# First scores ahead of the keys' second part, whole gathered rows scaled, and one last scatter, in a fused attention and MoE kernel

## The chip, the cores and the metric

One of the eight cores of a Trainium2 chip runs the whole program. A core has five engines with an instruction queue each: TensorE (PE, matmul; its weight loads are listed as PEld), VectorE (DVE), ScalarE (ACT), GpSimd (POOL) and SyncE (SP, which here only issues transfers). The metric is the time of one execution in device microseconds (us). Lower is better.

## The reference

An attention with keys and values pooled over eight neighbours, and behind it a mixture of experts in which each token goes to one expert (cut):

```python
batch, n_heads, seq, head_dim = (8, 8, 576, 64)
k_p = k.reshape(B, H, Sp, pool, D).mean(axis=3)      # Sp = 72, pool = 8
v_p = v.reshape(B, H, Sp, pool, D).mean(axis=3)
scores = scale * np.matmul(q, k_p.transpose(0, 1, 3, 2))
attn = softmax(scores)
x = np.matmul(attn, v_p)                             # as [4608 tokens, 512]
...
logits = x @ w_gate + modality_bias[modality_id]     # 8 experts
e_idx = np.argmax(logits, axis=1)
gate_w = softmax(logits)[arange(N), e_idx]
for e in range(E):                                   # w1 512x1024, w2 1024x512
    h = np.maximum(x[mask] @ w1[e], 0.0)
    out[mask] = gate_w[mask, None] * (h @ w2[e])
```

## The kernel before, in words

**Attention.** The 8 batches of 576 queries are worked through in 20 steps; each takes the rows of 256 tokens or so, five steps for every two batches, and has two halves of four heads (`sc_0`, `sc_1`). A half's life: query rows are transposed on PE (`pq`, L508) and copied by ACT (`qt`); PE makes the scores (`sc`, L533; L527 where a step spans two batches); DVE takes the maximum (`mx`, L540) and subtracts it (`sb`, L543); ACT takes the exponential (`pe`, L555, L556); PE transposes it (`pp`, L562, and `sc` L574 for the last columns) and ACT copies it (`pt`, L567, L581); PE multiplies with the pooled values (`av`, L597, L601), where the gate's logits and the sum of the exponentials come along as extra columns; DVE and ACT divide and write the rows (`xb`, L603 to L642); SP stores them to DRAM (`xs`).

Keys and values arrive in chunks (`c`) of 128 pooled rows and a rest `k4`, `v4`. The sum over eight neighbours is taken either by DVE in one reduction (`reduce8`, L309) or by POOL in three folding additions (`fold`, L304 to L306). PE transposes the key sums (`pk`, L340, L343) in two parts; `kt` is the scores' operand. The values' sums become `vw`, an operand for `av`.

The order of all this is written by hand. A prologue issues the loads on SP's queue and does the first sums and transposes; then each step runs a fixed sequence on PE, with places (`hook_0` to `hook_3`, `hook_q`) at which the next batch's sums and operands are called. Every engine works its own queue in that order, so an instruction that waits holds all behind it. The program before makes the first scores behind both parts of the keys of batch 0, and all key sums of batch 1's first part plus the second part's stand together on DVE.

In the late groups (the route is computed in four groups of steps; two are early) half of each token row is copied raw by ACT and is divided only after gathering, by POOL, the other half by DVE at once. The divisors travel in the row as extra columns.

**Experts.** Tokens are sorted by expert into slots of 256 rows, 18 fixed and up to 27 if the data need it; slots from index 18 on are under conditions (`more`, L1267 to L1285). With these data 19 slots are used and the last has 109 rows, so that a shorter end (`end_half`) runs. A slot: POOL gathers the two tiles of 128 rows from DRAM (`xg`, L143, an indirect DMA), multiplies half of each row by its divisors (`scale_half`, L148 to L153), PE transposes the rows (`xt`, L155 to L164). Then eight blocks f = 0 to 7 of 128 hidden units: PE makes `hp` (L170), ACT and DVE the rectified `hh` and its remainder `hlo`, PE the output `op` (L1155); meanwhile ACT and DVE split the next weights into two parts (`hl`, L136, L139). The results are scaled by the gate's weight into `ob` (DVE, ACT; L1132 to L1143) and scattered by POOL to `out` (L1141), which is done in the next slot's f = 0. Gathers for the next slot are issued there too, slot 2's at f = 3 of slot 1, behind slot 0's scatters. Scale and transposes come at f = 3 and f = 5 (slot 1: 5 and 6).

**End.** Behind the conditions stand two scatters of the rows in `obl` (L1288 to L1291), the first of them zeros when the last slot is half full. Each waits for the other's landing. Then the program ends (L1317).

Of the kernel before, what the change touches and what calls it, by code (L numbers as in the profile page):

```python
# [22 lines left out]
P = 128  # L23
# [7 lines left out]
def kernel(  # L31
# [116 lines left out]
    def scale_half(s, xgs):  # L148
        for tt in range(2):
            x = xgs[(2 * s + tt) % len(xgs)]  # L150
            xv = x[:, 0:D // 2].rearrange("p (h d) -> p h d", h=H // 2)
            nc.gpsimd.tensor_tensor(xv, xv, x[:, RX:RX + H // 2].rearrange("p (h o) -> p h o", o=1).to_broadcast([P, H // 2, HD]),  # L152
                                    op=ALU.mult)  # L153
# [37 lines left out]
    with ExitStack() as actx:  # L191
# [64 lines left out]
        load_q(0, (1,))  # L256
        load_v(0)
        load_v4(0)
# [55 lines left out]
        def pool_k(b, parts=(0, 1)):  # L314
# [5 lines left out]
            for i in parts:  # L320
                cs = K_PART[i]
                if b == 0 or (b == 1 and i == 0):
# [4 lines left out]
                else:  # L327
                    for c in range(cs[0], cs[-1] + 1, 2):
                        m = min(c + 2, cs[-1] + 1)
                        fold(t[:, c:m], kp[:, c:m])  # L330
                    if i == 1:
                        fold(t4, kp4)

        def k_operand(b, i):
# [4 lines left out]
            for j, c in enumerate(cs):  # L339
                nc.tensor.transpose(pk[:, j * P:(j + 1) * P], kp[:, c, :], ident)  # L340
            n = len(cs) * P
# [7 lines left out]
        def pool_v(b):  # L349
            vp = ap.tile([P, NPAIR, HD], F32, tag="vp", bufs=2, name=f"vp_{b}")  # L350
            vp4 = ap.tile([P, HD], F32, tag="vp4", bufs=2, name=f"vp4_{b}")
            t, t4 = vraw[b], v4raw[b]
            fold(t[:, 0:2], vp[:, 0:2])
            if b:
                fold(t[:, 2:4], vp[:, 2:4])
            else:
                for j in range(2, NPAIR):
                    reduce8(t[:, j, :], vp[:, j, :])
            fold(t4, vp4)
            vps[b] = (vp, vp4)  # L360

# [241 lines left out]
        def x_dve(t):  # L603
# [5 lines left out]
            if gi == 0:  # L609
# [7 lines left out]
            late = g >= EARLY_GROUPS  # L617
# [8 lines left out]
            nc.vector.tensor_tensor(xo[:, D // 2:D].rearrange("p (h d) -> p h d", h=4),  # L626
                                    avv[:, 1, :, 0:HD], rb[:, 1].to_broadcast([P, 4, HD]), op=ALU.mult)
            if late:
                nc.scalar.copy(xo[:, 0:D // 2].rearrange("p (h d) -> p h d", h=4), avv[:, 0, :, 0:HD])
            else:  # L630
                nc.vector.tensor_tensor(xo[:, 0:D // 2].rearrange("p (h d) -> p h d", h=4),
                                        avv[:, 0, :, 0:HD], rb[:, 0].to_broadcast([P, 4, HD]), op=ALU.mult)
# [180 lines left out]
        for n, (b, jj, _) in enumerate(steps):  # L813
            if b + 1 < B:
                if jj == 0:
                    m = n if b else n + 1
                    at(hook_0, m, lambda b=b: pool_v(b + 1))
                    at(hook_1, m, lambda b=b: k_operand(b + 1, 0))
                    at(hook_1 if b == 0 else hook_q if b % 2 else hook_3, m, lambda b=b: k_operand(b + 1, 1))
# [42 lines left out]
        load_q(1, (0,))  # L862
        load_q(1, (1,))
# [20 lines left out]
        q_act(0, 0)  # L884
        pool_k(0, (1,))
        token_ids()
# [3 lines left out]
        s_pe(0, 0)  # L890
        s_dve(0, 0)
        pool_v(0)
        gate_operand()
        s_act(0, 0)
        q_pe(1, 0)
        q_act(1, 0)
# [10 lines left out]
        for n in range(N + 1):  # L907
# [29 lines left out]
            if n == 0:  # L937
                v_operand(0)
# [25 lines left out]
            if n == 0:  # L964
                pool_k(1)
            run(hook_2, n)
# [6 lines left out]
            if n == 0:  # L973
                v_gate(0)
# [150 lines left out]
    def part(s):  # L1125
# [6 lines left out]
        def evac(tts=(0, 1)):  # L1132
            for tt in tts:
# [7 lines left out]
                nc.gpsimd.indirect_dma_start(  # L1141
                    out=out[:, :], out_offset=IndirectOffsetOnAxis(idx.bitcast(U32), 0),
                    in_=ob, in_offset=None, bounds_check=NTOK - 1, oob_is_err=False)  # L1143
# [44 lines left out]
        def run(fs, tail):  # L1188
            for f in fs:
                if f:  # L1190
                    hidden(f)
                if f == 0:
                    tail()
                    if nxt and s >= EARLY_SLOTS:
# [6 lines left out]
                if s == 1 and f == 3:  # L1201
# [4 lines left out]
                if f == (5 if s == 1 else 3) and nxt and not early:  # L1206
                    scale_half(s + 1, xg)
                if f == (6 if s == 1 else 5) and nxt:
# [6 lines left out]
        def last_rows(tt):  # L1215
            gt = xg[(2 * s + tt) % 4][:, D:D + 1]
            if tt == 0:
                nc.vector.tensor_scalar_mul(obl[0], o[0], gt)
            else:
                nc.scalar.activation(obl[1], o[1], AF.Copy, scale=gt)  # L1220

        def end(f0):

            nc.vector.tensor_copy(sl, sidx[:, 2 * s:2 * s + 2])
# [6 lines left out]
            last_rows(1)  # L1231
            for f in range(f0, NF):
                second(f, (0,), at[f])
            last_rows(0)

        def end_half(f0):

            nc.vector.tensor_copy(sl, sidx[:, 2 * s:2 * s + 2])
            nc.vector.memset(obl[1], 0.0)
# [6 lines left out]
            last_rows(0)  # L1246
# [6 lines left out]
    obl = [mp.tile([P, D], F32, name=f"obl{z}") for z in range(2)]  # L1253
    sl = mp.tile([P, 2], I32, name="sl")
# [33 lines left out]
    for tt in (1, 0):  # L1288
        nc.gpsimd.indirect_dma_start(
            out=out[:, :], out_offset=IndirectOffsetOnAxis(sl[:, tt:tt + 1].bitcast(U32), 0),  # L1290
            in_=obl[tt], in_offset=None, bounds_check=NTOK - 1, oob_is_err=False)  # L1291
# [30 lines left out]
```

## Time and profile before

| | us |
|---|---|
| median of 3 runs | 634.19 (633.3 to 634.3) |
| the profiled execution | 631.66 |
| its span | 629.9 |

The profiled execution has its own time and span: the span runs from the first to the last instruction in the trace, and 1.8 us of the time lie around it. Its mean granted TensorE clock is 0.992. Where the prediction speaks of the end, the program's last instruction ends at 629.9. All times of the trace count from the span's start. The attention lasts until about 200 us, the rest belongs to the experts; one expert slot is 20 to 25 us long. In the lists of groups, waits and timeline, "L152" is line 152 of the kernel, `out<-in` are the program's names, `[0.4 <-DMA q]` is how long the engine was idle before the instruction and what ended it. PEq, POOLq and so on are the engines' sequencers.

### The profile page before, as it was taken

Reading aid. Unit: us, or ns where it says so; the run is one execution under the profiler, and the core shown is the slowest. Engines: PE = TensorE matmul, PEld = TensorE weight load, DVE = VectorE, ACT = ScalarE, POOL = GpSimd, SP = SyncE. Lnnn points to the kernel's source line nnn. Section 1 sums busy time; section 2 is a strip of 40 time slices with the busy share of each in tenths; the row PEclk is TensorE's granted clock in tenths of the full one; section 3 lists DMA queues with packets and bytes.
Section 4 is the critical chain, followed back from the end, with each engine's and each line's share of the span. In section 5 each row is a group of like instructions: output and inputs, shape, how many; then the busy total and the mean of one; then the engine's idle time right before and its main releaser. Section 6 shows DMA issues by size and latency. Waiting matters only on the chain.

```text
span 629.9 us, 12488 instructions
## 1 busy us (share of the span) xinstructions
PE 601.1 (95%) x4223; PEld 544.8 (86%) x4223; DVE 409.1 (65%) x802; ACT 347.6 (55%) x666; POOL 237.8 (38%) x326
## 2 busy tenths in 40 slices
PE   4799999999999999999999999999999999999992
PEld 3699888897898898999999999999999999999991
DVE  4767888778957487656656566566566656656641
ACT  2667677887532555555555555555555555555540
POOL 5789968742000341331332331331331241331331
PEclk9899999999999999999999999999999999999997
DMA  9999969864113620120220460120135310120120
GB/s 252 308 284 350 355 199 362 261 209 137 53 70 110 227 69 17 52 69 7 64 69 16 153 223 31 50 68 18 53 91 183 132 56 18 53 69 18 52 70 19
DMA packets 63481, 77.12 MB, mean 122 GB/s; under 512 B 15535, under 2 KB 42159, under 8 KB 63408
## 3 DMA queue, kind: packets, MB, share of 16 engines
q1 hardware_dynamic: 57168, 55.98, 28.2%
q0 software_dynamic: 6240, 20.26, 10.0%
q8 instruction: 35, 0.57, 0.4%
q14 instruction: 38, 0.31, 0.2%
HBM read 119.94 MB, written 19.71 MB: 222 GB/s over the span
## 4 chain that ended last, share of the span: by engine, by line
PE 78%; DMA 6%; DVE 5%; issue 4%; ACT 3%; SPq 1%; POOL 1%; POOLq 0%; ACTq 0%; DVEq 0%
PE op L1155 29%; PE hp L170 29%; PE av L597 5%; PE sc L533 4%; PE av L601 2%; PE xt L161 2%; PE pq L508 2%; DMA out_dram<-ob,sidx 2%; PE pp L562 1%; PE ph L170 1%; DMA xg<-xs,gidx 1%; DMA k<-in_k_dram 1%; DMA raw<-in_moe_w_dram 1%; DVE kp L309 1%; DVE sb L543 1%
## 5 line engine op out<-in xcount | busy, mean ns | idle before, releaser
L136 ACT CAST hl<-raw 128x1024 fp32r<-128x1024 f32 x138 | 144.8, 1049 | 138.7 <-PE op L1155 134.7
L170 PE MATMUL hp<-xh,hl 128*128 128x256 f32 x1152 | 186.1, 284 | 0.0
L170 PEld LDWEIGHTS hp<-xh,hl 128*128 128x128 f32 x1152 | 166.1, 189 | 10.5
L139 DVE TENSOR_TENSOR hl<-raw,hl 128x1024 fp32r<-128x1024 f32 x144 | 175.0, 1217 | 0.0
L1155 PE MATMUL op<-hl,hh 128*128 128x512 f32 x554 | 173.5, 394 | 0.0
L1141 POOL DMA_INDIRECT out_dram<-ob,sidx x36 | 52.5, 1457 | 289.6 <-DVE ob L1137 184.5
L174 DVE SCALAR_TENSOR_TENSOR hlo<-hp,hh 128x256 fp32r<-128x256 f32 x139 | 58.7, 423 | 136.4 <-ACT hh L172 123.8
L1155 PE MATMUL op<-hl,hlo 128*128 128x512 f32 x277 | 108.4, 391 | 0.0
L1155 PEld LDWEIGHTS op<-hl,hh 128*128 128x128 f32 x554 | 94.8, 189 | 12.1
L170 PE MATMUL hp<-xl,hl 128*128 128x256 f32 x576 | 92.0, 282 | 0.0
L172 ACT ACTIVATE hh<-hp 128x256 fp32r<-128x256 f32 x139 | 53.3, 383 | 49.7 <-PE hp L170 47.8
L170 PEld LDWEIGHTS hp<-xl,hl 128*128 128x128 f32 x576 | 79.0, 190 | 0.0
L1155 PEld LDWEIGHTS op<-hl,hlo 128*128 128x128 f32 x277 | 52.0, 188 | 11.7
L597 PE MATMUL av<-vw,pt 128*128 128x146 f32 (+1 forms) x320 | 50.4, 297 | 1.4 <-ACT pt L567 0.9
L143 POOL DMA_INDIRECT xg<-xs,gidx x40 | 44.2, 1105 | 16.5 <-issue 10.4
L152 POOL TENSOR_TENSOR xg<-xg 128x256 f32<-128x256 f32 x34 | 31.2, 918 | 34.9 <-DMA xg<-xs,gidx 34.9
L597 PEld LDWEIGHTS av<-vw,pt 128*128 128x128 f32 (+1 forms) x320 | 40.3, 182 | 3.8 <-ACT pt L567 2.3
L533 PE MATMUL sc<-kt,qt 128*128 128x144 f32 x256 | 38.0, 292 | 0.0
L164 DVE TENSOR_TENSOR xl<-xt,xh 128x512 fp32r<-128x512 f32 x38 | 24.6, 685 | 17.1 <-ACT xh L163 17.1
L533 PEld LDWEIGHTS sc<-kt,qt 128*128 128x128 f32 x256 | 34.2, 195 | 0.2
L540 DVE TENSOR_REDUCE mx<-sc 128x8 f32<-128x576 f32 (+1 forms) x40 | 27.7, 692 | 10.0 <-PE sc L533 8.3
L601 PE MATMUL av<-vw,pt 128*128 128x146 f32 (+1 forms) x160 | 30.7, 295 | 0.4
(236 smaller groups left out, 713.0 us busy)
## 6 DMA issues: line engine op xcount, KB each, us to landing
raw<-in_moe_w_dram SPq DMA_DIRECT2D x304, 256.0 KB
xs<-xb SPq DMA_DIRECT2D x16, 528.0 KB
k<-in_k_dram SPq DMA_DIRECT2D x7, 1024.0 KB
v<-in_v_dram SPq DMA_DIRECT2D x7, 1024.0 KB
q<-in_q_dram SPq DMA_DIRECT2D x6, 1024.0 KB
q<-in_q_dram SPq DMA_DIRECT2D x4, 512.0 KB
v<-in_v_dram SPq DMA_DIRECT2D x16, 128.0 KB
xs<-xb SPq DMA_DIRECT2D x8, 132.0 KB
```

Of the source, the lines that this page charges most:

```text
L136: nc.scalar.copy(hl[f][:, 0, :], raw[f])
L139: eng.tensor_sub(hl[f][:, 1, :], raw[f], hl[f][:, 0, :].bitcast(F32))
L143: nc.gpsimd.indirect_dma_start(out=xgs[(2 * s + tt) % len(xgs)], out_offset=None, in_=xs[0:rows, :], in_offset=IndirectOffsetOnAxis(idx[:, ...
L152: nc.gpsimd.tensor_tensor(xv, xv, x[:, RX:RX + H // 2].rearrange("p (h o) -> p h o", o=1).to_broadcast([P, H // 2, HD]), op=ALU.mult)
L170: nc.tensor.matmul(ph, hl[f][:, w, d * P:(d + 1) * P], x[:, d, :], start=(n == 0 and d == 0), stop=(n == 2 and d == ND - 1))
L172: nc.scalar.activation(hh, ph, AF.Relu)
L174: nc.vector.scalar_tensor_tensor(hlo, ph, 0.0, hh.bitcast(F32), op0=ALU.max, op1=ALU.subtract)
L533: nc.tensor.matmul(dst, qt[:, i, :], kt[b % NB][:, :, h * SPL:(h + 1) * SPL], start=True, stop=True)
L597: nc.tensor.matmul(av[hs, u, 2 * VC * gg:2 * VC * (gg + 1)], pt[:, c, hs], vw[y][:, c].rearrange("p a x -> p (a x)"), start=(gg == 0), sto ...
L601: nc.tensor.matmul(dst4[hs], pt4[:, hs], v4[y][:, 2 * u:2 * u + 2, :], start=False, stop=True)
L1141: nc.gpsimd.indirect_dma_start(out=out[:, :], out_offset=IndirectOffsetOnAxis(idx.bitcast(U32), 0), in_=ob, in_offset=None, bounds_check=N ...
L1155: nc.tensor.matmul(o[tt], l[:, ts_], hl[f][:, w, D:2 * D], start=(f == 0 and n == 0), stop=(f == NF - 1 and n == 2))
```

## The change

**Loads.** q of batch 0 is loaded by heads, two transfers with rows of 1024 B instead of 512 B; q of batch 1 in one; v's rest `v4` ahead of v.

**Front.** `s_pe(0, 0)` and `s_dve(0, 0)` (the first scores, their maximum and subtraction) come ahead of the keys' second part and of the token indices. A new function `fill` puts 58 dummy bf16 matmuls into PE's queue, 20+5+5 between the first transposes of keys, then 6, 14 and 8. Sums of batch 1: POOL folds c0 and c1 of k, DVE sums c2 in step 0 and c3 in step 1 (`pool_k_rest`); of v, POOL folds three chunks and DVE sums c3 (`pool_v_rest`, batches 1 and 2). The key operands of batch 1 move to `hook_q` and to `hook_2` of step 1, behind the first step's `av`.

On DVE before, the piece from the first `sb` of step 1 to the first rows of `av` (`kp` key sums of batch 1, `mx`/`sb` maximum and subtraction of scores, `r`, `xb` division and rows of `av`):

```order
L543 TENSOR_TENSOR sb_0_334<-sc_0_327,mx_0_332 128x576
L309 TENSOR_REDUCE kp_336<-k_191 128x64 x3
L540 TENSOR_REDUCE mx_1_418<-sc_1_392 128x8
L543 TENSOR_TENSOR sb_1_420<-sc_1_392,mx_1_418 128x576
L620 TENSOR_SCALAR r_439<-av_411 128x8
```

The same place in the program after:

```order
L565 TENSOR_TENSOR sb_0_397<-sc_0_390,mx_0_395 128x576
L309 TENSOR_REDUCE kp_408<-k_191 128x64
L562 TENSOR_REDUCE mx_1_468<-sc_1_453 128x8
L565 TENSOR_TENSOR sb_1_470<-sc_1_453,mx_1_468 128x576
L642 TENSOR_SCALAR r_495<-av_461 128x8
L644 RECIPROCAL r_495<-r_495 128x8
L646 TENSOR_TENSOR lg_494<-av_461,r_495 128x64
L652 TENSOR_TENSOR xb_167<-av_461,r_495 128x256 x2
L562 TENSOR_REDUCE mx_0_516<-sc_0_504 128x2x2
L565 TENSOR_TENSOR sb_0_518<-sc_0_504,mx_0_516 128x2x144
L309 TENSOR_REDUCE kp_408<-k_191 128x64
```

Of the three sums one is left in its place, one has moved behind the first `av` rows and step 2's first maximum, and one has left DVE.

On PE before, from the second half's scores of step 1 (`sc_1`) on (`pk` key transposes, `av` values, `pp` transposed exponentials):

```order
L533 MATMUL sc_1_392<-kt_133,qt_1_318 128x2x72 x4
L574 MATMUL sc_0_327<-ident,pe_277 128x128
L340 MATMUL pk_0_400<-ident,kp_336 64x128 x3
L340 MATMUL pk_1_406<-ident,kp_336 64x128
L343 MATMUL pk_1_406<-ident,kp_1_337 64x64
L597 MATMUL av_411<-vw_137,pt_387 128x146 x2
L601 MATMUL av_411<-vw_139,pt_0_135 128x2x73
```

The same after:

```order
L555 MATMUL sc_1_453<-kt_133,qt_1_381 128x2x72 x4
L596 MATMUL sc_0_390<-ident,pe_340 128x128
L619 MATMUL av_461<-vw_137,pt_448 128x146 x2
L623 MATMUL av_461<-vw_139,pt_0_135 128x2x73
L619 MATMUL av_461<-vw_137,pt_448 128x146 x2
L623 MATMUL av_461<-vw_139,pt_0_135 128x2x73
L584 MATMUL pp_472<-ident,pe_340 128x128 x4
L530 MATMUL pq_0_480<-ident,qm_195 128x128 x2
L530 MATMUL pq_1_485<-ident,qm_195 128x128 x2
L349 MATMUL pk_0_488<-ident,kp_408 64x128 x3
L549 MATMUL sc_0_504<-kt_133,qt_0_479 64x144
```

The values of the first half now stand ahead of the transposes of the new keys; these stand behind the query transposes of step 2, and their second part (not in the rows) behind step 2's first scores.

**Rows.** In the late groups the two 128-row tiles of a step are treated apart: tile 0 is divided by DVE, tile 1 is copied raw and whole by ACT. POOL scales the whole gathered row of 512 columns (`scale`), with divisors of 1 for rows that are divided already.

**Slots.** In slot 1 the gather of slot 2 comes at f = 2, ahead of slot 0's scatters, and these wait in a list (`later`) until the scale at f = 4 has been issued. In the slots of index 17 and above, the gathers stand behind the condition at f = 3, so that two gathers that nobody uses are not made. At f = 4 of slot 16 (index), POOL drains: `nc.gpsimd.drain()`.

**End.** Behind the conditions only one scatter is left, of one tile `obl` whose halves DVE and ACT write one after the other. On POOL before (`obl`, `sl`: rows and indices of the last scatters):

```order
L1280 ISA
L1272 UNCONDITIONAL_BRANCH
L1289 DMA out_dram<-obl_2805,sl 4608x512
L1289 DMA out_dram<-obl_2804,sl 4608x512
L1317 UNCONDITIONAL_BRANCH
L1317 ISA
```

The same after:

```order
L1169 DMA out_dram<-ob_1_10966,sidx 4608x512
L1321 ISA
L1313 UNCONDITIONAL_BRANCH
L1329 DMA out_dram<-obl,sl 4608x512
L1357 UNCONDITIONAL_BRANCH
L1357 ISA
```

The tt = 1 rows' scatter (L1169) now belongs to the full-length end inside the condition; one stands behind it.

The diff, cut to its core:

```diff
-    def scale_half(s, xgs):
+    def scale(s, xgs):
...
-            xv = x[:, 0:D // 2].rearrange("p (h d) -> p h d", h=H // 2)
+            xv = x[:, 0:D].rearrange("p (h d) -> p h d", h=H)
...
-            if b < 2:
+            if b == 0:
                 for i in parts:
-                    nc.sync.dma_start(dst[:, :, 2 * HD * i:2 * HD * (i + 1)], src[:, :, 2 * HD * i:2 * HD * (i + 1)])
+                    nc.sync.dma_start(dst[:, 4 * i:4 * i + 4], src[:, 4 * i:4 * i + 4])
...
+                        if b == 1 and c == 2:
+                            reduce8(t[:, c, :], kp[:, c, :])
+                        elif b > 1 or c < 2:
+                            fold(t[:, c:m], kp[:, c:m])
...
+        def fill(n):
+            t = ps_av.tile([P, 2, 512], F32, tag="av", name="fill")
+            for _ in range(n):
+                nc.tensor.matmul(t[:, 0, 0:P], iota_b, iota_b, start=True, stop=True)
...
+        def pool_k_rest(b):
+            reduce8(kraw[b][:, 3, :], kps[b][0][:, 3, :])
...
-            late = g >= EARLY_GROUPS
+            late = g >= EARLY_GROUPS and z == 1
...
             if late:
-                nc.scalar.copy(xo[:, 0:D // 2].rearrange("p (h d) -> p h d", h=4), avv[:, 0, :, 0:HD])
+                nc.scalar.copy(xo.rearrange("p (u h d) -> p u h d", u=2, h=4), avv[:, :, :, 0:HD])
...
         q_act(0, 0)
+        fill(6)
+        s_pe(0, 0)
+        fill(14)
         pool_k(0, (1,))
+        s_dve(0, 0)
         token_ids()
         k_operand(0, 1)
...
-                if s == 1 and f == 3:
+                if s == 1 and f == 2:
+                    gather(s + 1, gidx, 2 * (s + 1), xg)
+                if s >= NSTAT - 1 and f == CUT and nxt:
                     gather(s + 1, gidx, 2 * (s + 1), xg)
...
+                if s == NSTAT - 2 and f == 4:
+                    nc.gpsimd.drain()
...
-    for tt in (1, 0):
-        nc.gpsimd.indirect_dma_start(
-            out=out[:, :], out_offset=IndirectOffsetOnAxis(sl[:, tt:tt + 1].bitcast(U32), 0),
-            in_=obl[tt], in_offset=None, bounds_check=NTOK - 1, oob_is_err=False)
+    nc.gpsimd.indirect_dma_start(
+        out=out[:, :], out_offset=IndirectOffsetOnAxis(sl.bitcast(U32), 0),
+        in_=obl, in_offset=None, bounds_check=NTOK - 1, oob_is_err=False)
```

More of the change, by code (lines that the diff above doesn't have):

```diff
@@ L340, in k_operand @@
                 nc.tensor.transpose(pk[:, j * P:(j + 1) * P], kp[:, c, :], ident)
+                if b == 0 and i == 0:
+                    fill(5 if j else 20)
             n = len(cs) * P
@@ L1140, in evac, with put @@
                 idx = (sidx0 if s < EARLY_SLOTS else sidx)[:, 2 * s + tt:2 * s + tt + 1]
-                nc.gpsimd.indirect_dma_start(
-                    out=out[:, :], out_offset=IndirectOffsetOnAxis(idx.bitcast(U32), 0),
-                    in_=ob, in_offset=None, bounds_check=NTOK - 1, oob_is_err=False)
+                def put(ob=ob, idx=idx):
+                    nc.gpsimd.indirect_dma_start(
+                        out=out[:, :], out_offset=IndirectOffsetOnAxis(idx.bitcast(U32), 0),
+                        in_=ob, in_offset=None, bounds_check=NTOK - 1, oob_is_err=False)
+                if later is None:
+                    put()
+                else:
+                    later.append(put)
         def hidden(f, at=None):
@@ L1188, in run @@
         def run(fs, tail):
+            later = []
             for f in fs:
@@ L1192, in run @@
                 if f == 0:
-                    tail()
-                    if nxt and s >= EARLY_SLOTS:
+                    if s == 1:
+                        tail(later=later)
+                    else:
+                        tail()
+                    if nxt and EARLY_SLOTS <= s < NSTAT - 1:
                         gather(s + 1, gidx, 2 * (s + 1), xg)
@@ L1205, in run @@
                     renew(f - 1)
-                if f == (5 if s == 1 else 3) and nxt and not early:
-                    scale_half(s + 1, xg)
-                if f == (6 if s == 1 else 5) and nxt:
+                if f == (3 if EARLY_SLOTS <= s < NSTAT - 1 else 4) and nxt and not early:
+                    scale(s + 1, xg)
+                    while later:
+                        later.pop(0)()
+                if s == NSTAT - 2 and f == 4:
+                    nc.gpsimd.drain()
+                if f == (5 if EARLY_SLOTS <= s < NSTAT - 1 else 6) and nxt:
                     x_transposes(s + 1, xg)
@@ L1213, in run, with last_rows @@
                     renew(f)
[L1215 to L1220, printed above, removed]
+        def last_rows():
+            gt = xg[2 * s % 4][:, D:D + 1]
+            nc.vector.tensor_scalar_mul(obl[:, 0:D // 2], o[0][:, 0:D // 2], gt)
+            nc.scalar.activation(obl[:, D // 2:D], o[0][:, D // 2:D], AF.Copy, scale=gt)
         def end(f0):
-            nc.vector.tensor_copy(sl, sidx[:, 2 * s:2 * s + 2])
+            nc.vector.tensor_copy(sl, sidx[:, 2 * s:2 * s + 1])
             at = {f: hx[f - f0] for f in range(f0, NF)}
@@ L1251 @@
     hx = [[mp.tile([P, SLOT], F32R, name=f"hx{i}_{z}") for z in range(2)] for i in range(NF - CUT)]
-    obl = [mp.tile([P, D], F32, name=f"obl{z}") for z in range(2)]
-    sl = mp.tile([P, 2], I32, name="sl")
+    obl = mp.tile([P, D], F32, name="obl")
+    sl = mp.tile([P, 1], I32, name="sl")
     lag = []
```

59 lines of the change are left out of this document (32 added, 27 removed).

## The prediction

> **What bounds the kernel now.** I read the page first: the busy times, then the span in 40 slices (busy tenths of PE, and the clock that it was granted).
>
> ```profile
> PE 601.1 (95%) x4223; PEld 544.8 (86%) x4223; DVE 409.1 (65%) x802; ACT 347.6 (55%) x666; POOL 237.8 (38%) x326
> PE   4799999999999999999999999999999999999992
> PEclk9899999999999999999999999999999999999997
> ```
>
> PE (TensorE) is busy in 95% of the span and all the middle slices are full. The change removes no matmul that counts there; what it can win lies in the first two slices (4, 7) and the last (2), each slice being 15.7 us, and in single waits of PE between. So I looked next at PE's waits in three stretches: 0 to 30, 30 to 200 and 200 to 600 us.
>
> ```profile
> PE pk L340 <- DVE kp L309: 8.8, 6, 4.9
> PE xt L161 <- POOL xg L152: 0.7, 1, 0.7
> ```
>
> The first row is of 0 to 30: PE waits 8.8 us for the key sums that VectorE (DVE) makes. The second is the only wait of the stretch 200 to 600. Then the windows of the front, whose columns are length, busy time of PE, PEld, DVE, ACT, POOL, clock, DMA share, GB/s:
>
> ```profile
> 5.00:10.00 5.00, 2.23 (x7) 0.97 (x6) 2.47 (x3) 1.53 (x3) 2.95 (x25) 1.00 1.06 281
> 20.00:25.00 5.00, 3.24 (x23) 2.33 (x22) 4.90 (x7) 2.85 (x12) 3.38 (x7) 1.00 1.08 320
> 25.00:30.00 5.00, 4.54 (x22) 4.12 (x21) 2.27 (x7) 2.41 (x6) 4.62 (x7) 0.66 1.11 338
> ```
>
> DVE is full from 20 to 25 us (4.90 of 5); PE becomes full in the third of these, under a granted clock of 0.66. Ahead of 30 us DVE sets the pace, after it PE does. The gain of the front is therefore how much earlier PE's unbroken work begins.
>
> **The front: DVE loses work.** The timeline of 8 to 33 us (start, length, engine, line, operation):
>
> ```profile
> 8.22 1.11 PE L508 MATMUL pq<-ident,q 128*128 128x128 f32 x4 [0.40 <-DMA q<-in_q_dram]
> 12.34 2.12 PE L533 MATMUL sc<-kt,qt 128*128 128x144 f32 x8
> 15.11 1.14 PE L533 MATMUL sc<-kt,qt 128*128 128x144 f32 x8
> 14.50 0.76 DVE L540 TENSOR_REDUCE mx<-sc 128x8 f32<-128x576 f32 x1 [2.56 <-PE sc L533]
> 15.29 0.76 DVE L543 TENSOR_TENSOR sb<-sc,mx 128x576 f32<-128x576 f32 x1
> 15.97 1.99 DVE L309 TENSOR_REDUCE vp<-v 128x64 f32<-128x512 f32 x2
> 15.89 0.73 POOL L304 TENSOR_TENSOR v<-v 128x256 f32<-128x256 f32 x1 [0.37 <-DMA v<-in_v_dram]
> 21.70 2.89 DVE L309 TENSOR_REDUCE kp<-k 128x64 f32<-128x512 f32 x3
> 24.65 0.41 PE L340 MATMUL pk<-ident,kp 128*64 128x128 f32 x2 [0.63 <-DVE kp L309]
> 25.16 1.20 PE L597 MATMUL av<-vw,pt 128*128 128x146 f32 x4
> 22.62 0.55 ACT L581 COPY pt<-sc 64x128 f32<-64x128 f32 x2
> 31.20 0.66 PE L597 MATMUL av<-vw,pt 128*128 128x146 f32 x4
> ```
>
> The same eight score matmuls take 2.12 us at 12.34 and 1.14 at 15.11, and four of L597 take 1.20 at 25.16 and 0.66 at 31.20: PE is slow in its first work and again around 25 us. The 58 dummy matmuls are put where PE waits. With the scores ahead of the keys' second part, they can start about 1.2 us after pq's end (8.22+1.11, and an ACT copy behind it), at 10.5 instead of 12.34, and if the dummies keep PE fast they take 1.1: end 11.6. The maximum and the subtraction (0.76 each) are then over at 13.2, before the values' second part arrives; POOL's row says that the last values land at about 15.9. Before, DVE came to the values at 15.97, so this part alone brings 0.1 to 0.6, the latter if rows of 1024 B let everything land half a microsecond sooner; I take 15.4. From there DVE's order is the old one, up to the keys of batch 1: vp to 17.4, maximum and subtraction of the next half to 18.9, vw to 19.7, the next pair to 21.25. Of the three key sums (2.89, so 0.96 each) only one stays here; POOL folds two. Before, the first L597 stood behind L340 and so behind all three; now it stands ahead of the keys and waits for the probabilities' copy (22.62 before, 22.0 now): it can begin at 22 instead of 25.16, three microseconds sooner.
>
> That is not kept whole. The last key sum now stands on DVE behind the next step's maximum and subtraction: first L597 group 22 to 23.7, the row work on DVE to 25.5, the scores of step 2 on PE to 27, maximum and subtraction to 28, the sum to 28.9. PE's transpose of it, and the second L597 group behind it, begin at 29.0, with a new wait of about 1.3 us on PE. Before, the second group began at 31.20. **Front: −2.2 us**; 0 if the dummies take as long as the transposes beside them (1.11/4 = 0.28 each, so 8 ahead of the next scores cost 2.2) and −3.1 if the sum is early enough.
>
> The Trainium skill, "DMA: Bandwidth & Descriptors" (Specifications), puts line rate at transfers of 512 B or more: by it the rows of 1024 B win nothing, v lands at 15.9, and the front would be −1.7. The trace speaks rather against it: 281 GB/s in 5 to 10 us, while q's rows of 512 B move, against 338 in 25 to 30, with longer rows.
>
> **Rows of the late groups.** For half of them DVE does one more multiplication and ACT one copy less, for the other half the reverse:
>
> ```profile
> 28.92 0.41 DVE L626 TENSOR_TENSOR xb<-av,r 128x256 f32<-128x256 f32 x1
> PE av L597 <- DVE xb L631: 0.4, 1, 0.4
> ```
>
> 0.41 us more or less per step; PE's waits of 30 to 200 us name DVE's rows once, with 0.4. POOL's folds change places too, but the front's end is set by DVE. I take 0, with ±0.5.
>
> **The gather of slot 2.** In slot 1, the timeline of 200 to 222 us:
>
> ```profile
> 208.34 1.47 POOL L1141 DMA_INDIRECT out_dram<-ob,sidx  x1 [5.86 <-DMA raw<-in_moe_w_dram]
> 210.12 1.04 POOL L143 DMA_INDIRECT xg<-xs,gidx  x1 [0.30 <-DMA raw<-in_moe_w_dram]
> 216.27 1.60 POOL L152 TENSOR_TENSOR xg<-xg 128x256 f32<-128x256 f32 x1 [1.12 <-DMA xg<-xs,gidx]
> 217.93 0.66 PE L161 MATMUL xt<-ident,xg 128*128 128x128 f32 x4 [0.71 <-POOL xg L152]
> ```
>
> The gather stands behind slot 0's scatters, and POOL was idle for 5.86 us ahead of the second of them; now the gather goes at f=2, ahead of them, and they go behind the scale. It can leave at least the 1.47 of that scatter earlier, so the scale is done when PE comes: **−0.7**, the whole wait of the second row above. The scatters that are deferred hold nothing: nobody reads their rows.
>
> **Whole rows to scale, in slots 2 to 17.** POOL now multiplies 512 columns where it did 256. Nearest rows: slot 17's, and a small one of the same kind.
>
> ```profile
> 22.52 0.23 POOL L397 TENSOR_TENSOR vw<-vg,m 128x32 f32<-128x32 f32 x1
> 590.22 0.61 POOL L152 TENSOR_TENSOR xg<-xg 128x256 f32<-128x256 f32 x1 [0.44 <-DMA xg<-xs,gidx]
> 591.30 1.03 PE L161 MATMUL xt<-ident,xg 128*128 128x128 f32 x8
> L152 POOL TENSOR_TENSOR xg<-xg 128x256 f32<-128x256 f32 x34 | 31.2, 918 | 34.9 <-DMA xg<-xs,gidx 34.9
> ```
>
> From 32 to 256 columns is 0.38 us, so 512 columns are 0.61+0.43 = 1.04 undisturbed. Here the scale would end at 591.26 instead of 590.83, with PE's transposes at 591.30: just in time, and of eight transposes the second row tile is needed only by the last four, half of 1.03 us later. So I take 0. If the tile is late by all that is added, and the mean (0.92 against 0.61) shows that scales already wait or stretch, a slot pays up to 0.75; below 0 it can't go, as PE doesn't wait there now.
>
> **The end.** The last rows, issues and the program's end:
>
> ```profile
> 617.86 0.75 DVE L1218 TENSOR_SCALAR obl<-op,xg 128x512 f32<-128x512 f32 x1 [0.60 <-PE op L1155]
> 184.74 0.37 ACT L629 COPY xb<-av 128x256 f32<-128x256 f32 x1 [2.19 <-DVE xb L626]
> 621.63 1.00 POOL L1289 DMA_INDIRECT out_dram<-obl,sl  x1 [2.71 <-DMA out_dram<-obl,sl]
> 617.91 2.94 DMA out_dram<-obl,sl
> L1317 POOLq DRAIN  x3: 40/113/7685, 621.4 to 629.7; - x3
> L1317 POOLq EVENT_SEMAPHORE  x4: 17/17/17, 629.1 to 629.8; - x4
> ```
>
> Before, the real scatter is issued at 621.63, since it waits for the landing of another that here carries only zeros (617.91+2.94 and some queue work). Now one is left. Its rows are made by DVE and then ACT, half each: 617.86+0.41+0.37 = 618.64, with a gap each 618.9: issue at 618.96, **−2.7**. POOL has nothing else in front of it by then: the two useless gathers that followed slot 18's are behind a condition now. Bounds: −3.1 if the halves run side by side, −1.9 if each handover takes 0.6, as the one from PE to DVE in the first row.
>
> Behind the issue POOL's queue drains for 7.685 us, to 629.1. The scatter's issue ends at 622.63, it lands at 621.63+2.94 = 624.57, so the drain lasts 4.5 us beyond the landing; nothing else moves then. I read it as work per software transfer: 6.46 us behind the issue for 78 transfers.
>
> ```profile
> xg<-xs,gidx POOLq DMA_INDIRECT x40, 3.7
> out_dram<-ob,sidx POOLq DMA_INDIRECT x36, 3.7
> out_dram<-obl,sl POOLq DMA_INDIRECT x2
> 578.61 1.78 POOL L1141 DMA_INDIRECT out_dram<-ob,sidx  x1 [12.29 <-DVE ob L1137]
> ```
>
> 40+36+2 = 78, 0.083 us each. The new drain in slot 16 takes the first 70 or so, while POOL has nothing to do: it is idle for 12.29 us before 578.61. Seven are left at the end, 0.6 us, less than the landing needs. Then the program ends 0.8 us behind the landing, as before behind the drain (629.9−629.1): 618.96+2.94+0.8 = 622.7 without the other terms. **−4.5**, 0 if the drain's length is fixed. If the cover in slot 16 is too short (over 12 us), slot 16's scatters are late, and nobody waits for them but the buffers of ob, of which there are four.
>
> **Sum.** −2.2 −0.7 +0 +0 −2.7 −4.5 = −10.1 on the profiled execution: 631.66 to 621.6. The three timed runs have a median of 634.19, 2.5 above it; I carry the difference over: 624.1.
>
> **The rivals.** *Drain of fixed length.* For it: the profile has only this one long drain, and no row says what it does in its 7.685 us. Against: it goes on 4.5 us after the last landing, when nothing is moving. The end then gives only −2.7: 628.6.
>
> *The front brings nothing.* The dummies delay the scores, or the clock falls again: it was 0.66 in 25 to 30 us right after a stretch (20 to 25) with PE busy for 3.24 of 5 us, and the new wait on the last key sum is such a gap. At half speed the first L597 groups take 1.20 instead of 0.66 each, and all that PE does for some 4 us twice as long: that eats the 2.2, and the time is 626.3. The Trainium skill, "TensorE: Matmul & The Clock Gate" (Part 1), lets PE's clock rise after some 3.4 us of sustained work and judges it in windows that run free of the program. It gives 107 ns for a slow matmul of 128 columns, so the first 30 dummies would be an estimated 3.2 us, just short of such a window; this rival would be likelier by it than the rows of before, which have no dummies, can say.
>
> *Half of the slots pay a little.* The scale is late in about seven slots by 0.7: +5, 629.
>
> *Slower: POOL's scale sets the pace.* Place: the transposes of L161 in slots 2 to 17, which come no later than before while each of POOL's tiles costs 0.43 more. The scale of 216.27, with DVE at work beside it, took 1.60, 2.6 times the 0.61 of another. If the second tile is late by 0.75 us in every slot (0.43, and the 0.3 by which the mean scale exceeds 0.61), 16 slots cost 12 us: 636.1. The sign turns at 10.1/16 = 0.63 us per slot. Against it: PE's only wait there is 0.7 us in the whole stretch.
>
> **How the numbers follow.** Forecast 0.52, fixed drain 0.24, front nothing 0.14, some slots 0.06, slower 0.04. The forecast's own range is 622.2 to 626.0 (front −0.5 to −3.1, end ±0.7, rows ±0.5). For 8 in 10 it must reach over the fixed drain with its own uncertainty of 1.6: 630.2 above; below 621.5. A measurement of this kernel can tell 0.2%, 1.3 us. Faster by more: all but the last case and a share of "some slots", 0.93; within 0.03; slower 0.04.
>
> **What the profile after would show.** Right: scores at about 10.5 and the second L597 group at 29 us; no wait on POOL in PE's waits from 200 to 600; one scatter behind the conditions, issued at 618.96 − 2.2 − 0.7 = 616.1; the end's drain over with the landing, and a long one (5 us or more) in slot 16. Wrong: the end's drain again over 6 us; a clock below 1 at 25 to 30 us with the second L597 group at 31 or later; a row "xt <- POOL xg" with ten times or more.

## The result, and the profile after

| | before | changed |
|---|---|---|
| median, us | 634.19 (632.4 to 634.3, 5 runs) | 626.88 (625.41 to 627.32, 5 runs) |
| profiled execution, us | 631.66 | 626.88 |
| its span, us | 629.9 | 625.2 |

The ratio is 0.9885 with a 95% interval of 0.9867 to 0.9903: 7.3 us faster, where 10.1 were forecast. The profiled execution of before is a short one of its kind, so the two profiled executions show only 4.8 us of it. 626.88 lies 0.9 us above the forecast's own range, and inside the wide one only because that range was stretched to reach a rival, the fixed drain, which the runs below rule out.

The page after, the same two rows over 40 slices as shown of before (PE busy, granted clock):

```profile
PE   6699999999999999999999999999999999999996
PEclk9999999999999999999999999999999999999999
```

The first slices went from 4 and 7 to 6 and 6, and the last from 2 to 6. The end is the plain part. Its rows after, from the timeline of 609 to 626 us (POOL's row is the issue of the one scatter left):

```profile
619.69 0.48 DVE L1261 TENSOR_SCALAR obl<-op,xg 128x256 f32<-128x256 f32 x1 [0.60 <-PE op L1187]
620.21 0.47 ACT L1262 ACTIVATE obl<-op,xg 128x256 f32<-128x256 f32 x1 [1.58 <-DVE obl L1261]
620.96 0.97 POOL L1329 DMA_INDIRECT out_dram<-obl,sl  x1 [12.56 <-ACT obl L1262]
```

And the drains by line (L1250 is the new one in slot 16, L1357 the program's end; shortest, median and longest in ns, then the starts of the first and last):

```profile
L1250 POOLq DRAIN  x1: 7212/7212/7212, 567.0 to 567.0; - x1
L1357 POOLq DRAIN  x3: 46/113/3292, 620.7 to 624.9; - x3
```

From the start of the last rows' scaling to the span's end there were 12.1 us before (617.86 to 629.94), now there are 5.5 (619.69 to 625.16): 6.6 less, against 7.2 forecast. The scatter is issued 1.27 us behind that start instead of 3.77. The drain at the end takes 3.3 us instead of 7.7, and 7.2 us of draining stand in slot 16.

But the last rows begin at 619.69, 1.8 us later than before, where 2.9 us earlier were forecast. Slot 0's first transposes, a mark near the end of the attention, start at 155.57, where they started at 155.46: the front has won nothing by then, and the other 1.7 us are lost in the expert slots. PE's first work shows the lead that was won and lost (timeline of 8 to 34 us):

```profile
10.33 1.22 PE L555 MATMUL sc<-kt,qt 128*128 128x144 f32 x8 [0.43 <-ACT qt L536]
15.82 1.98 DVE L309 TENSOR_REDUCE vp<-v 128x64 f32<-128x512 f32 x2 [1.33 <-DMA v<-in_v_dram]
22.20 0.66 PE L619 MATMUL av<-vw,pt 128*128 128x146 f32 x4
27.12 0.70 PE L549 MATMUL sc<-kt,qt 128*64 128x144 f32 x6 [0.66 <-ACT kt L358]
28.79 1.02 DVE L309 TENSOR_REDUCE kp<-k 128x64 f32<-128x512 f32 x1
29.76 1.02 PE L530 MATMUL pq<-ident,q 128*128 128x128 f32 x4 [1.94 <-DMA q<-in_q_dram]
31.16 1.34 PE L619 MATMUL av<-vw,pt 128*128 128x146 f32 x4
```

The scores come at 10.3 and the first values at 22.2, as forecast. Then PE waits 1.94 us for q of batch 1, a wait that was not there before, and the second values start at 31.16, where they started at 31.20. The last key sum ends at 29.81, nearly when q lands, and not at the 28.9 of the prediction: the scores of step 2 wait 0.66 us for ACT's copy of the new keys and end at 27.8 instead of 27, and the sum stands behind them on DVE. The second values also take 1.34 instead of 0.66. Windows of 3.4 us beside each other show why, before and after (columns as in the prediction: length, PE, PEld, DVE, ACT, POOL, clock, DMA share, GB/s):

```profile
18.50:21.90 3.40, 3.20 (x28) 3.05 (x27) 3.26 (x6) 3.01 (x11) 2.42 (x5) 1.00 1.13 288
21.90:25.30 3.40, 1.84 (x12) 1.01 (x11) 3.35 (x4) 1.57 (x6) 1.98 (x4) 1.00 1.12 304
25.30:28.80 3.50, 3.50 (x16) 3.49 (x17) 1.15 (x4) 1.25 (x4) 3.19 (x6) 0.51 1.11 331
```

```profile
23.00:26.40 3.40, 2.94 (x21) 2.16 (x21) 2.06 (x7) 1.16 (x4) 2.74 (x6) 1.00 1.08 314
26.40:29.80 3.40, 0.81 (x8) 0.51 (x8) 1.84 (x4) 1.76 (x5) 3.16 (x5) 1.00 1.06 374
29.80:33.30 3.50, 3.50 (x15) 3.00 (x16) 0.98 (x2) 1.10 (x3) 1.78 (x4) 0.51 1.06 282
```

In both, PE has a window with long waits (the second row before, the second row after), and in the next one it works without a gap at half clock. After, the idle window is emptier (0.81 us of work) and comes later.

In the expert slots, PE's waits of 200 to 640 us name POOL's scale twice:

```profile
PE xt L161 <- POOL xg L152: 2.3, 2, 1.2
```

The gather of slot 2 did its part: its transposes run as one piece.

```profile
216.64 1.03 PE L161 MATMUL xt<-ident,xg 128*128 128x128 f32 x8
```

The two waits are in later slots, at 381 and 429 us, and make 2.3 us against the wait of 0.7 that went. The prediction had no wait on POOL there.

### The profile page after: what moved, and what is told of

Same layout as the page of the kernel before. It is cut to its first block, busy times and chain, and to the rows that moved or that the text cites. A ratio compares the mean times of both kernels' runs of the same rounds, so it can differ in the third digit from the quotient of the medians.

```text
span 625.2 us, 12575 instructions
## 1 busy us (share of the span) xinstructions
PE 603.2 (96%) x4281; PEld 547.7 (88%) x4281; DVE 413.4 (66%) x804; ACT 347.5 (56%) x657; POOL 248.6 (40%) x323
## 4 chain that ended last, share of the span: by engine, by line
PE 75%; DMA 8%; issue 7%; DVE 5%; POOL 2%; ACT 2%; SPq 1%; POOLq 0%; DVEq 0%; ACTq 0%
PE hp L170 28%; PE op L1187 28%; PE av L619 5%; DMA q<-in_q_dram 3%; PE sc L555 3%; DMA xg<-xs,gidx 2%; PE av L623 2%; PE xt L161 2%; DMA out_dram<-ob,sidx 2%; PE pq L530 2%; PE pp L584 2%; POOL xg L152 2%; PE ph L170 1%; DVE hl L139 1%; DVE sb L565 1%
## 5 line engine op out<-in xcount | busy, mean ns | idle before, releaser
L139 DVE TENSOR_TENSOR hl<-raw,hl 128x1024 fp32r<-128x1024 f32 x144 | 177.9, 1237 | 0.0
L1169 POOL DMA_INDIRECT out_dram<-ob,sidx x36 | 51.5, 1429 | 225.8 <-DVE ob L1163 173.6
L1187 PEld LDWEIGHTS op<-hl,hh 128*128 128x128 f32 x554 | 94.8, 189 | 12.1
L152 POOL TENSOR_TENSOR xg<-xg 128x512 f32<-128x512 f32 x34 | 45.8, 1352 | 30.8 <-DMA xg<-xs,gidx 30.7
L619 PE MATMUL av<-vw,pt 128*128 128x146 f32 (+1 forms) x320 | 50.1, 296 | 1.4 <-ACT pt L589 1.1
L589 ACT COPY pt<-pp 128x512 f32<-128x512 f32 x36 | 21.1, 586 | 17.8 <-PE pp L584 17.3
```

The source lines that it names most:

```text
L139: eng.tensor_sub(hl[f][:, 1, :], raw[f], hl[f][:, 0, :].bitcast(F32))
L152: nc.gpsimd.tensor_tensor(xv, xv, x[:, RX:RX + H].rearrange("p (h o) -> p h o", o=1).to_broadcast([P, H, HD]), op=ALU.mult)
L619: nc.tensor.matmul(av[hs, u, 2 * VC * gg:2 * VC * (gg + 1)], pt[:, c, hs], vw[y][:, c].rearrange("p a x -> p (a x)"), start=(gg == 0), sto ...
L1169: nc.gpsimd.indirect_dma_start(out=out[:, :], out_offset=IndirectOffsetOnAxis(idx.bitcast(U32), 0), in_=ob, in_offset=None, bounds_check=N ...
L1187: nc.tensor.matmul(o[tt], l[:, ts_], hl[f][:, w, D:2 * D], start=(f == 0 and n == 0), stop=(f == NF - 1 and n == 2))
```

## The experiments

Twelve kernels ran, in three groups of four. The medians of before beside them were 634.02, 633.93 and 633.70. The changed kernel itself was not run again beside them, so a difference to its 626.88 by the medians carries these 0.5 us and more; the ratios are the safer comparison. Half-clock stretches and the time of full clock are read from each profile's granted clock. Its record begins when the clock becomes full; ahead of that the windows print 1.00, although PE is slow there (the first scores of before, 2.12 us at 12.34).

| kernel | median, us | ratio to before, 95% |
|---|---|---|
| before + drain in slot 16 | 629.17 | 0.9931 [0.9907, 0.9955] |
| before + one last scatter | 630.70 | 0.9952 [0.9937, 0.9967] |
| before + slots and end | 626.13 | 0.9887 [0.9864, 0.9910] |
| before + front | 634.30 | 1.0020 [0.9998, 1.0041] |
| changed, front as before | 625.43 | 0.9874 [0.9847, 0.9901] |
| the same + 44 dummies | 626.32 | 0.9887 [0.9862, 0.9911] |
| changed, no drain in slot 16 | 630.17 | 0.9933 [0.9908, 0.9958] |
| changed, half rows | 627.08 | 0.9889 [0.9859, 0.9919] |
| changed, q of batch 1 sooner | 626.83 | 0.9885 [0.9856, 0.9915] |
| changed, 30 dummies at 28 us | 624.97 | 0.9873 [0.9847, 0.9900] |
| both of the last two | 625.94 | 0.9874 [0.9845, 0.9903] |
| changed, no dummies | 624.02 | 0.9843 [0.9815, 0.9871] |

### The drain, added and taken away

To before:

```diff
+                if s == NSTAT - 2 and f == 4:
+                    nc.gpsimd.drain()
```

> The kernel before, with the one drain on POOL at f = 4 of slot 16 added and nothing else. Theory (the end's drain works off what was transferred since the last drain, 0.083 us each): some 72 of 78 transfers are worked off in slot 16 under PE's work, the drain at the end falls from 7.7 us to about 3 and ends with the last landing: 4.4 us less, about 629.8 against 634.2, and a drain of 5 to 6 us shows in slot 16. Rival (the end's drain has a fixed length, and the gain of the changed kernel's end comes from having one scatter less): the time stays within 1 us of 634.2 and the end's drain stays over 6 us. The trace is also a second look at the expert slots of the kernel before: if PE's waits on POOL's scale there are an accident of the run and not of the row's width, waits of 1 us or more show here too.

The same two lines taken from the changed kernel:

> The changed kernel without the drain in slot 16. Theory (work per transfer): the end's drain grows from 3.3 us to about 7.5, the time from 626.9 to about 631.3. Rival (fixed length): within 1 us of 626.9.

629.17 and 630.17: 4.9 us less with it in the one kernel, 3.3 more without it in the other. The drains of the first (in slot 16, and at the end), then that at the end of the second:

```profile
L1209 POOLq DRAIN  x1: 6298/6298/6298, 566.8 to 566.8; - x1
L1319 POOLq DRAIN  x3: 46/112/3704, 622.5 to 626.9; - x3
```

```profile
L1355 POOLq DRAIN  x3: 40/113/7420, 621.9 to 630.0; - x3
```

The drain's length is not fixed. It is worked off in slot 16, and PE shows no wait there, or later, in the profiles of before + drain and of the changed kernel. That the work is 0.083 us for each transfer can be read too, since the drains stand behind four different numbers of indirect transfers. The drain of slot 16 is entered while the second scale still runs (in the changed kernel at 567.04):

```profile
567.07 1.52 POOL L152 TENSOR_TENSOR xg<-xg 128x512 f32<-128x512 f32 x1 [0.46 <-DMA xg<-xs,gidx]
```

So its length of 6.3 to 7.9 us holds the rest of the scale. Counted from the end of POOL's last work ahead of it, the scale or the last scatter's issue, each long drain ends after:

| drain | transfers since the start | us | us each |
|---|---|---|---|
| slot 16, all ten kernels with it | 68 | 5.65 | 0.083 |
| end, changed, no drain in slot 16 | 75 | 6.21 | 0.083 |
| end, before + one last scatter | 77 | 6.38 | 0.083 |
| end, before, and before + front | 78 | 6.46 | 0.083 |

With only 7 or 10 transfers left for the end, its drain goes on for 2.0 to 2.5 us behind the issue, more than 0.083 each would make. In the changed kernel the scatter lands 1.7 us behind the issue's end, and the drain ends 0.3 us behind the landing.

The profile of before + drain was also a second look at the slots of before: PE's only wait on the scale is slot 2's, 0.7 us.

### One last scatter alone

With it go its rows, made half by DVE and half by ACT as in the change (cut):

```diff
-    for tt in (1, 0):
-        nc.gpsimd.indirect_dma_start(... sl[:, tt:tt + 1] ..., in_=obl[tt], ...)
+    nc.gpsimd.indirect_dma_start(... sl ..., in_=obl, ...)
```

> The kernel before with one last scatter only, no drain in slot 16. Theory (the issue comes 2.5 us sooner and the end's drain follows 6.4 us behind the issue, for 77 transfers): 631.5, with an end's drain of over 7 us. Rival (the two gains hide each other: the drain works off old transfers while it waits for the last, so an earlier issue brings nothing without the drain in slot 16): 634.

630.70, 3.2 us less. From the start of the last rows' scaling to the span's end there are 9.5 us instead of 12.1, and the end's drain is as long as ever:

```profile
L1314 POOLq DRAIN  x3: 40/113/7630, 621.1 to 629.3; - x3
```

The two savings at the end add up in the spans (2.6 and 4.0 alone, 6.6 together); neither hides the other.

### The slots and the end without the rest, and the front alone

Before with the diff's pieces from the expert part (gathers, drain, end), half rows kept:

> The kernel before with the slots' and the end's part alone: slot 2's gather earlier, useless gathers dropped, drain in slot 16, one last scatter; front and half rows as before. Theory: all of the gain is here, 4.4 + 2.5 + 0.8 = 7.7 us, 626.3, no slower than the whole change. Rival (front and rows carry 2 us of it): 628.5.

Before with the pieces of the attention's front, nothing behind it:

> The kernel before with the changed front alone (loads, first scores, dummies, batch 1's sums and operands); rows, slots and end as before. Theory (q of batch 1 lands at about 30 us and PE, idle for it, falls into windows of 3.4 us at half clock, each 1.7 us of work lost; so the lead of 3 to 4 us at the first values is gone by 35 us): no gain, 0 to +1 us, about 634.5. Rival (the prediction's front: the lead is worth 2.2 us and other runs show it): 631.8.

The changed kernel with these front pieces taken back:

> The changed kernel with the front of before; rows, slots, drain and end as changed. Theory (front worth nothing or a little less): 626 to 627, the same as the changed kernel. Rival (front worth 2.2 us): 629.

626.13, 634.30 and 625.43. The slots and the end give all of the gain (a ratio of 0.9887, against 0.9885 for the whole change): the front alone is no gain (−0.1 to +2.6 us by its interval), and without it the changed kernel is 1.4 us faster by the medians, 0.7 by the ratios, with intervals that overlap (a little below the 626 to 627 expected). In the profile of the front alone, q of batch 1 is there in time, and PE waits for the key sum behind it:

```profile
29.00 0.65 PE L530 MATMUL pq<-ident,q 128*128 128x128 f32 x4
31.20 0.27 PE L349 MATMUL pk<-ident,kp 128*64 128x128 f32 x1 [1.55 <-DVE kp L309]
31.57 1.00 PE L619 MATMUL av<-vw,pt 128*128 128x146 f32 x4
```

That is the wait that the prediction had named, 1.3 us on the last key sum, about two microseconds later than placed. The wait for q and this one are alternatives: whichever ends later holds PE.

### q of batch 1 sooner

Its load is split in two again, and the order of the loads is (cut):

```diff
+        load_q(1, (0,))
         load_v(1)
         load_v4(1)
-        load_q(1)
+        load_q(1, (1,))
```

> The changed kernel with q of batch 1 loaded in two halves as before, the first of them ahead of v of batch 1 and the second behind it. Theory (the front's lead of 3 to 4 us is lost because PE waits until 29.8 us for q of batch 1, which lands late as one transfer behind v): the wait of 1.9 us goes, the second group of values starts at about 29 us or sooner instead of 31.2, and 1 to 2 us of it are left at the end of the attention: 625 to 626. Rival 1 (all loads of the front come one behind the other at the rate of the memory, so v of batch 1, now 1.7 us later, becomes the next wait): PE waits on the values of batch 1 or the keys of batch 2 instead, and the time stays within 0.5 us of 626.9. Rival 2 (the clock is what costs): the granted clock falls below 0.9 between 25 and 40 us here too, and no more than 0.5 us is won.

626.83: nothing. The wait for q is gone, and behind it stands the one for the key sum:

```profile
28.54 0.66 PE L533 MATMUL pq<-ident,q 128*128 128x128 f32 x4
30.74 0.27 PE L352 MATMUL pk<-ident,kp 128*64 128x128 f32 x1 [1.55 <-DVE kp L312]
31.12 1.34 PE L622 MATMUL av<-vw,pt 128*128 128x146 f32 x4
```

The second values start at the same 31.1, again at half clock (31.1 to 34.5). So q is not the cause by itself; two waits lie side by side, and neither the theory nor rival 1 had this one as the next. Rival 2 is right that the clock falls here too.

### Half rows again

Here `x_dve` and the scale are taken back to those of before (two tiles half raw, 256 columns to scale).

> The changed kernel with the rows of the late groups as before: both tiles half raw, half divided, and POOL scales half rows of 256 columns after gathering. Theory (the whole rows of 512 columns make POOL's scale late in some slots, three waits of PE of about 1.2 us each in the profile): PE's waits on POOL's scale in the expert part go to 1 us or less in all, and the time falls by 2 to 3 us, to about 624.3. Rival (the waits come from gathers that land late in some slots whatever the width): waits of 1 us or more remain, and the time stays within 0.7 us of 626.9.

627.08: no gain, as the rival had it, so whole rows are not what was lost. PE's waits on the scale are 0.7 us in this profile. But they come and go with whole rows too: they are absent in the profiles of five other kernels with whole rows, and present in that of the front-alone kernel, which has half rows. In the slot at 381 us, first the changed kernel, then the front alone:

```profile
379.34 1.92 POOL L152 TENSOR_TENSOR xg<-xg 128x512 f32<-128x512 f32 x1 [0.90 <-DMA xg<-xs,gidx]
381.32 0.66 PE L161 MATMUL xt<-ident,xg 128*128 128x128 f32 x4 [1.16 <-POOL xg L152]
```

```profile
382.28 1.39 POOL L152 TENSOR_TENSOR xg<-xg 128x256 f32<-128x256 f32 x1 [1.39 <-DMA xg<-xs,gidx]
383.72 0.66 PE L161 MATMUL xt<-ident,xg 128*128 128x128 f32 x4 [0.73 <-POOL xg L152]
```

Where the gathered rows land late, PE waits 0.73 us with half rows and 1.16 with whole ones: 0.43 for the width, just the price that the prediction had from two rows. Where they land in time, the width costs nothing. Of the 14 profiles, five have such a late gather in one or both of these two slots; why it is late in some executions only stays open.

### The dummies

All 58 away:

```diff
         def fill(n):
-            t = ps_av.tile([P, 2, 512], F32, tag="av", name="fill")
-            for _ in range(n):
-                nc.tensor.matmul(t[:, 0, 0:P], iota_b, iota_b, start=True, stop=True)
+            return
```

> The changed kernel with none of its 58 dummy matmuls. Theory (the dummies bring the clock to full at 8 to 10 us instead of 14 to 17, but that time is waited for again at 28 to 31 us): the first scores take 2.1 us instead of 1.2, the first values come later than 22.2, and the time stays within 1 us of 626.9. Rival (the dummies carry what the front brings, or cost): 1.5 us or more to one side.

624.02 (622.03 to 624.83), the lowest median of all, and 2.9 us less than the changed kernel (2.7 by the ratios, whose intervals barely overlap; all five runs lie below all five of the changed kernel): the rival is right, on the side of a cost. The first scores are slow again, and yet the first values come at 22.74, half a microsecond later than with the dummies:

```profile
10.20 2.26 PE L553 MATMUL sc<-kt,qt 128*128 128x144 f32 x8 [0.77 <-ACT qt L534]
```

The other way round, 44 dummies in the old front:

> The changed kernel with the order and loads of the front as before, but with 44 dummies (30 between the first transposes of keys, 14 behind the first query transposes). Theory (an earlier full clock alone doesn't move DVE's work, which sets the pace until 25 us): the first scores take 1.1 us instead of 2.1, and the time is the same as without the dummies, 625.4, within 0.8. Rival (the cold clock was what the front lost): 623.5 to 624.5.

626.32, 0.9 us slower than without by the medians, a little more than the theory's 0.8, with intervals that overlap; nothing is won, as the theory had it, though for more than its reason. The first scores take 1.15 us and still start at 12.24; but a later group of the same eight, with the window around it, is slow:

```profile
19.50 2.07 PE L541 MATMUL sc<-kt,qt 128*128 128x144 f32 x8
```

```profile
15.00:20.00 5.00, 2.22 (x10) 1.84 (x11) 3.76 (x5) 3.28 (x10) 3.22 (x9) 0.80 1.16 262
```

The first values come at 26.62, 1.6 us later than without them (25.04).

What the dummies do to the clock shows over all 14 profiles. With them PE is at full clock from 8 to 11 us on, without them from 14 to 18. With them, five of eight profiles have a half-clock stretch that starts between 11 and 20 us; without them, none of six. The timed runs agree: the mean of their granted clocks is 0.994 in the changed kernel and 0.997 without its dummies, 0.992 in the old front with dummies and 0.997 without.

I read it so: PE waits at 15 to 18 us for the values of batch 0, with or without dummies; a PE that became fast at 9 us is slowed for it, one that became fast at 15 is not yet. That fits four of the five stretches, which start at 18.0 to 19.4; the fifth starts at 11.3, behind an earlier window of waits (PE busy for 1.7 of 3.4 us).

The cost in time is less sure than the clock. The two profiled executions, with all dummies and without any, have no such stretch; slot 0's transposes start at 155.57 and 155.94, and what parts them is the two late gathers of the former. A stretch at 19 to 25 us falls on the scores through which DVE's chain runs, as in the half-row profile, where slot 0's transposes start at 160.3:

```profile
20.00:25.00 5.00, 5.00 (x24) 4.86 (x23) 2.46 (x3) 2.56 (x9) 2.19 (x3) 0.50 1.06 298
```

### 30 more dummies where PE waits at 28 us

```diff
+            if n == 1:
+                fill(30)
             if nxt2 and n > 0:
                 q_pe(n + 2, 0)
```

> The changed kernel with 30 more dummies where PE waits for q of batch 1 and the last key sum of batch 1, at about 28 us (2.0 us at the 0.067 us that the changed kernel's dummies take). Theory (the wait there leaves one window of 3.4 us nearly idle, and the next goes at half clock): no half-clock window between 28 and 40 us in the profile, and 1.7 us or a little less won: 625.2 to 625.8. Rival (the windows come for another reason, or the dummies hold PE as long as they save): a half-clock window there all the same, or 626.5 to 627.5.

624.97 (622.05 to 627.25), 1.9 us less than the changed kernel by the medians, with intervals that overlap. The profiled execution, the fastest of its runs, has no half-clock stretch ahead of the program's end (timeline, and the window of 30 to 35 us):

```profile
27.55 1.85 PE L341 MATMUL fill<-iota_b 128*128 128x128 bf16 x30
30.16 0.77 PE L619 MATMUL av<-vw,pt 128*128 128x146 f32 x4
```

```profile
30.00:35.00 5.00, 5.00 (x44) 4.57 (x44) 2.67 (x8) 3.59 (x11) 4.13 (x7) 1.00 1.04 322
```

The second values start 1.0 us sooner than in the changed kernel and run at full clock; the first transposes of slot 0, a mark near the end of the attention, come at 153.5 instead of 155.6. Over the profiles: a half-clock stretch starts between 29.8 and 32.5 us in all six kernels with the changed order of the front and no dummies at this place, in neither of the two that have them there, and in none of the six with the old order. So in these profiles the wait lets the clock fall, and work put into it holds it up, though in two of two only. By the ratios the kernel is 0.8 us faster than the changed one, and that gain is not shown to be other than zero.

### Both

> The changed kernel with the first half of q of batch 1 ahead of v of batch 1 and 30 more dummies in the wait for the last key sum behind it. Theory: both the wait for q and the half-clock window of 28 to 40 us go: 624.5 to 625.5. Rival (the loads set when the keys and values of the next batches come, whatever PE does): PE waits for them later, and the time stays at 626.5 to 627.

625.94: neither as good as the theory has it nor at the rival's end. In the profile there is no half-clock stretch at 30 us, but one of 6.8 us at 19.4, as in other kernels with the early dummies. The values of batch 0 were waited for 1.9 us there, and the start at 33.87 of the second values shows the whole front late.

## Why the prediction was right or wrong, point by point

**The end, −2.7 and −4.5.** Right, by mechanism and nearly by size. One scatter less is −2.5 in the timeline (3.77 to 1.27 us), and −2.6 in the span of the kernel that has this alone. The drain alone leaves 8.1 us behind the start of the last rows' scaling instead of 12.1: −4.0. Both together are −6.6, where −7.2 were forecast: the issue comes 1.27 us behind the start of the scaling instead of 1.1, and the program ends 1.5 us behind the landing (620.96 + 2.7 to 625.16) instead of 0.8. The rival of a fixed drain fell, and the 0.083 us for each transfer hold.

**The gather of slot 2, −0.7.** Right: the wait is gone in every profile with the edit, and the stretch from the first transposes of slot 0 to the last rows' scaling is 461.3 to 461.5 us in the six such profiles without a wait of PE on the scale, against 462.4 before: −1.0. In the changed kernel's own profile it is 464.1, for the two late gathers.

**Whole rows, 0 (up to 0.75 a slot).** Right on the whole. A late gather shows the price of 0.43, but in two slots at most, so the slower rival (16 slots) did not come. The sign of being right, no wait on POOL from 200 to 600 us, did not come either: 2.3 us stand there, which half rows would have as well, less 0.43 a slot.

**The front, −2.2.** This is the step that failed. "The second L597 group behind it, begin at 29.0 … Before, the second group began at 31.20. Front: −2.2 us": it began at 31.16, and the front alone is worth nothing (+0.4 by the median). The values' first group was forecast right at 22. Three things were missing. q of batch 1 lands at 29.7, as one transfer; its landing was never read, and PE waits 1.94 us for it. The last key sum ends at 29.8 instead of 28.9 (at 31.05 with the front alone), behind scores that wait for the copy of the new keys. And the clock: the window of waits leaves 3.4 us at half clock behind it, 1.7 us of PE's work. The rival "the front brings nothing" named that wait and the fall of the clock, and had it at 626.3; the time was 626.88. It got a chance of 0.14, and should have had more, since the windows of before showed the same step, from a window with waits to one at half clock.

**Dummies.** The prediction gave them the gain of early scores and, as their own cost, the time that they take. The runs showed another: they begin PE's fast time earlier than its work can keep it. Without them the changed order of the front may be worth something: 624.02 against 625.43 with the old order, but with intervals that overlap, so it is not shown.

**The sum.** 0 from the front, −1.0, −2.6 and −4.0 are −7.6; measured −7.3. The way and most of the size were forecast right, by the two terms of the end. The 626.3 of the front's rival is the forecast without its front, and nearly that came.

**Rows of 1024 B, and the clock.** The Trainium skill, "DMA: Bandwidth & Descriptors" (Specifications), had it that rows of 1024 B win nothing over 512 B. The trace agrees as far as it goes: the values land at 15.8 us, as before. The Trainium skill, "TensorE: Matmul & The Clock Gate" (Part 1), has a half and a full clock, judged in windows of some 3.4 us. The profiles agree: each half-clock stretch of the attention shows 0.50 and lasts 3.4 or 6.8 us.

## What to carry to other kernels

A lead won on one engine ahead of a load lasts only until the next transfer that the lead now waits for: read the landings of everything that the sped-up chain will ask for next, not only of what it asked for before. A wait of PE can cost twice, once as itself and once as half speed behind it, here 1.94 us and up to 1.7. Dummies kept the clock up in the wait itself, and let it fall when they made PE fast ahead of a wait that was still to come; ask when the work can keep PE busy before putting them in. A drain of a queue of transfers at the end of a program can be paid earlier, under other work: here some 4 us.

## What the runs showed of the hardware that was not expected

- The times of one kernel spread by 2 to 6.5 us (630.6 to 636.7 over 17 runs of before). In the profiles, the number of half-clock windows differs from run to run in code that is the same up to there (one and three at the front of the changed kernel and of that without the drain), each worth up to 1.7 us of PE's work.
- Count windows of 3.41 us from the start of the clock's record, up to 90 us, in all 14 profiles: 311 at full clock. All 6 with PE busy for less than 1.5 us were followed by half clock, none of the 275 with more than 2.5, and 9 of the 30 between. So the busy time decides at both ends and not in the middle: 2.4 us were followed by half clock at 65.3 in the kernel with the old front, 1.8 were not at 15.1 in before. What decides there stays open.
- 30 bf16 dummies took 1.85 us, 0.062 us each; the first 20, from a slow PE, 2.34 us.
- The changed order without its 58 dummies, but with 30 in the wait at 28 us, is what these runs point to. It was not run.
